# Attention, then two gated layers, on one core: first loads in one queue, weights' clamp on GpSimd, weight steps counted by eight

## The chip, the core and the metric

The kernel runs on one core of a Trainium2 chip. The time is that of one execution in microseconds on the device, the median of 3 runs. The engines are called as in the profile: PE (TensorE, matmuls), DVE (VectorE), ACT (ScalarE), POOL (GpSimd), SP (SyncE, which only issues transfers here). POOL issues transfers too, in its own queue.

## What is computed

```python
# attention with decay: B, H, S, D = 4, 8, 768, 64, one gamma for each head
for t in range(S):
    state = gamma * state + k[:, :, t] (outer) v[:, :, t]
    y[:, :, t] = scale * q[:, :, t] @ state
x = y as 3072 tokens x 512
# first layer: w1, w2 512x1024, w3 1024x1024, w_out 1024x512
x = ((x @ w1) * (x @ w2)) @ w3 @ w_out
# second layer: w_in 512x2048, w_out 2048x512
h = x @ w_in
out = (h * sigmoid(1.702 * h)) @ w_out
```

q, k, v are float32, all weights float64.

## The kernel before

**Attention** runs over 24 chunks of 128 tokens, 6 for each of 4 sequences (class `Attention`). A chunk's q, k, v are one tile, 1.05 MB, loaded by POOL's queue (`load`); there are four such tiles, so the load for chunk c + 4 waits until chunk c is done with its own. For a chunk PE computes scores `s`, the state's update `u` and the output `y` (from the masked scores `pt`, and from the state where there is one). ACT scales v into `vs`; DVE masks the scores into `pt` and multiplies y by a decay factor `dy` into `xb`. The factors of chunk 0 are loaded, those of the other five places come from POOL as products (`factors`). The first four chunks stay in SBUF, split by ACT and DVE into a high and a low part (`xh`, `xl`); the others are stored (`xd`). Tile `y` has one buffer.

**Weights** come as float64, in halves of a tile, 0.52 MB each (`fetch`, tile `raw`, five buffers), and are turned on the chip into a float32 high and low part. That is a generator, `weight_steps`, one instruction of DVE to a step. For a tile: two clamps (L168), the two low parts of the tile ahead (L118), two shifts left (L175), two or-steps with the lower word (L179), two and-steps that set the sign (L188). ACT makes the magnitudes (`magnitude`, L109) and the high parts (L113). When an and-step has read a raw half for the last time, the next half is fetched. `PAIR_OPS` is the count of steps to a tile.

**The order** is written out by hand: `tc.manual_schedule` keeps each engine's instructions as the program gives them, and an engine that waits holds up all that is behind it in its queue. `run` walks over the chunks and calls `fill(c, at)` at four places in each; `fill` takes `OPS[...][at]` weight steps, 3 to a chunk until the four tiles of `w_out` and the first of `w3` are made, then 8. From then on it also puts a *mix block* behind a chunk's output, where a tile of w3 is ready: 24 matmuls (tile `psw`) that multiply one of 8 blocks of w3 with w_out in advance. Mix blocks that are left are done when attention has ended. The gate stage (tile `psm`, w1 and w2) comes next, and then the rest.

Of the kernel before, what the change touches and what calls it, by code (L numbers as in the profile page):

```python
# [9 lines left out]
I32 = mybir.dt.int32  # L10
AF = mybir.ActivationFunctionType
ALU = mybir.AluOpType
# [6 lines left out]
NCK = S // P  # L19
NC = B * NCK  # L20
# [6 lines left out]
R_BUFS = 5  # L27
# [5 lines left out]


LEAST, MOST = 2.0, (1 + 0x680000 / 2**23) * 2.0**32
PAIR_OPS = 10

OPS = (1, 0, 1, 1), (2, 2, 2, 2)

# [2 lines left out]
def tile_kernel(  # L42
# [14 lines left out]
    nc = tc.nc  # L57
# [26 lines left out]
    raws, wx, parts = {}, {}, {}  # L84
# [4 lines left out]
            homes[tag].tile([P, 1024], F32R, tag=tag, bufs=8, name=f"w{x}") for x in "hl"  # L89
        )  # L90

    def fetch(n):

        i, c = divmod(n, 2)
        if i >= len(tiles):
            return
        src = tiles[i][0][:, c * WC : (c + 1) * WC].bitcast(I32)
        raw = prep.tile([P, WC, 2], I32, tag="r", bufs=R_BUFS, name="raw")
        nc.sync.dma_start(raw, src.rearrange("p (c w) -> p c w", w=2))
        raws.setdefault(i, []).append(raw)  # L100

    def magnitude(i):
        if i >= len(tiles):
            return
        wx[i] = []
        for raw in raws[i]:
            x = prep.tile([P, WC], F32, tag="x", bufs=4, name="x")
            high = raw[:, :, 1].bitcast(F32)
            nc.scalar.activation(x, high, AF.Abs, scale=2.0**16)  # L109
            wx[i].append(x)  # L110

    def upper(i, n):
# [49 lines left out]
    def weight_steps():  # L162

        for i in range(len(tiles)):
            if i == 0:
                magnitude(i)
            for x in wx[i]:
                nc.vector.tensor_scalar(x, x, LEAST, MOST, ALU.max, ALU.min)  # L168
                yield i - 1
            for k, low in enumerate(lows):  # L170
                low()
                yield i - (k < len(lows) - 1)
            for x in wx[i]:
                bits = x.bitcast(I32)
                nc.vector.tensor_scalar(bits, bits, 3, None, ALU.logical_shift_left)  # L175
                yield i
            for x, raw in zip(wx[i], raws[i]):
                bits = x.bitcast(I32)
                nc.vector.scalar_tensor_tensor(  # L179
                    bits, raw[:, :, 0], 29, bits, ALU.logical_shift_right, ALU.bitwise_or  # L180
                )
                yield i
            magnitude(i + 1)
            if i < WI:
                parts[i] = wtile(tiles[i][1])
            for n, (x, raw) in enumerate(zip(wx[i], raws[i])):
                bits = x.bitcast(I32)
                nc.vector.scalar_tensor_tensor(  # L188
                    bits, raw[:, :, 1], -(2**31), bits, ALU.bitwise_and, ALU.bitwise_or
                )  # L190
                if i < WI:
                    upper(i, n)
                fetch(2 * i + n + R_BUFS)
                yield i
            if i < WI:
                lows[:] = [lambda i=i, n=n: lower(i, n) for n in range(2)]
            else:
                for _ in seven(i):
                    yield i
        for low in lows:  # L200
            low()
            yield i + 1
# [4 lines left out]
    def work(n):  # L207

        nonlocal complete, done
        for _ in range(n):  # L210
            complete = next(steps, len(tiles))
            done += 1
# [34 lines left out]
    class Attention:  # L247
# [121 lines left out]
        def run(self, fill):  # L369

            self.scores(0)
            self.masked(0)
            for c in range(NC):
                if c + 1 < NC:
                    self.scores(c + 1)
                fill(c, 0)
                if c + 1 < NC:
                    self.masked(c + 1)
                fill(c, 1)
                self.updates(c)  # L380
                self.next_state(c)
                if c + 3 < NC:
                    self.load(c + 3)
                if c + 2 in range(2, NCK):
                    self.factors(c + 2)
                fill(c, 2)
                self.outputs(c)
                fill(c, 3)


# [311 lines left out]
    with tc.manual_schedule():  # L702
        with (
# [3 lines left out]
            attention = Attention(p0, ps0)  # L707
            nc.sync.dma_start(attention.dv, cv)
            nc.sync.dma_start(attention.mask, cmask)
            fetch(0)  # L710
            attention.load(0)
            fetch(1)
            attention.load(1)
            nc.sync.dma_start(attention.step[:, :NCK], cstep)
            attention.factors(0)
            attention.load(2)
            attention.factors(1)
            for n in range(2, R_BUFS):
                fetch(n)
            psw = None  # L720
            halves_done = 0

# [30 lines left out]

            def fill(c, at):
                nonlocal usable
                work(OPS[usable > W3][at])
                mix_out()
                if at == 3 and W3 + halves_done // 2 < min(usable, W12):
                    mix_half()
                    mix_half()  # L760
                usable = complete

            work(3)
            attention.run(fill)
            while halves_done < 2 * KF:
                f = halves_done // 2
# [220 lines left out]
```

## Time and profile before

| | us |
|---|---|
| runs | 1027.65, 1027.82, 1028.16 |
| median | 1027.82 |
| the profiled execution | 1028.51 |
| its span, first to last instruction | 1026.7 |
| PE busy in it | 991.8 (97%) |
| DVE, ACT, POOL busy | 647.6, 441.8, 46.1 |

The profile is of one execution. A line of the timeline merges neighbours of one kind (x2: two instructions); what stands in brackets is the idle time of the engine just before, and what ended it. DMA share is the mean busy share of the 16 DMA engines, PEclk the granted clock of PE, 1.00 being full speed.

### The profile page before, as it was taken

What the parts mean: (1) busy time and instruction counts of PE and PEld (TensorE: products, weight loads), DVE (VectorE), ACT (ScalarE), POOL (GpSimd) and SP (SyncE); (2) the same over time, 40 slices, a digit from 0 to 9 for tenths busy, and PEclk for the clock granted to TensorE, in tenths of its full rate; (3) what the DMA queues carried; (4) which work ended last, traced back from release to release, by engine and by line L of the source; (5) the groups of instructions that cost most, each with busy time, mean ns of one, the idle gap of its engine ahead of it and who ended that gap; (6) DMA issues with size and microseconds to landing.
All of it is one profiled execution on the core that took longest, in us unless ns stands there. A gap on an engine that the chain in (4) does not pass through costs nothing.

```text
span 1026.7 us, 16851 instructions
## 1 busy us (share of the span) xinstructions
PE 991.8 (97%) x6688; PEld 900.1 (88%) x6688; DVE 647.6 (63%) x1048; ACT 441.8 (43%) x875; POOL 46.1 (4%) x65
## 2 busy tenths in 40 slices
PE   4879999999999999999999999999999999999997
PEld 3668777888888888888889999999999999999997
DVE  4877888856767777742442362634646588687782
ACT  4767544433434434322113455555455343433431
POOL 3110000000000000000001000000001011011011
PEclk9999999999999999999999999999999999999999
DMA  8999645436676666650137925233469854344331
GB/s 310 336 400 361 239 155 177 151 125 220 230 269 201 223 238 215 219 177 16 55 131 313 372 96 181 102 132 151 150 220 416 330 165 162 110 138 142 106 123 41
DMA packets 80159, 202.79 MB, mean 198 GB/s; under 512 B 6736, under 2 KB 33488, under 8 KB 75088
## 3 DMA queue, kind: packets, MB, share of 16 engines
q1 hardware_dynamic: 73888, 146.14, 40.8%
q0 software_dynamic: 6192, 55.58, 13.8%
q8 instruction: 52, 0.85, 0.3%
q14 instruction: 27, 0.22, 0.1%
HBM read 129.34 MB, written 72.35 MB: 196 GB/s over the span
## 4 chain that ended last, share of the span: by engine, by line
PE 87%; DMA 6%; DVE 4%; issue 1%; ACT 1%; POOL 0%; DVEq 0%; ACTq 0%; POOLq 0%
PE psm L225 8%; PE psm L224 8%; PE psm L223 8%; PE m L223 8%; PE m L225 8%; PE m L224 8%; PE acc L224 4%; PE acc L223 4%; PE acc L225 4%; DMA qkv<-in_qkv_dram 4%; PE a L223 4%; PE a L224 4%; PE a L225 4%; PE e L223 2%; PE e L224 2%; PE e L225 2%
## 5 line engine op out<-in xcount | busy, mean ns | idle before, releaser
L223 PE MATMUL m<-oh,op 128*128 128x256 f32 x672 | 188.2, 280 | 0.0
L225 PE MATMUL m<-oh,op 128*128 128x256 f32 x672 | 187.6, 279 | 0.0
L224 PE MATMUL m<-ol,op 128*128 128x256 f32 x672 | 187.6, 279 | 0.0
L225 PE MATMUL psm<-xh,wl 128*128 128x512 f32 x384 | 149.5, 389 | 1.2 <-DVE wl L118 1.2
L224 PE MATMUL psm<-xl,wh 128*128 128x512 f32 x384 | 149.4, 389 | 0.0
L223 PE MATMUL psm<-xh,wh 128*128 128x512 f32 x384 | 149.4, 389 | 0.0
L225 PEld LDWEIGHTS m<-oh,op 128*128 128x128 f32 x672 | 126.4, 188 | 0.0
L223 PEld LDWEIGHTS m<-oh,op 128*128 128x128 f32 x672 | 126.3, 188 | 0.0
L224 PEld LDWEIGHTS m<-ol,op 128*128 128x128 f32 x672 | 125.8, 187 | 0.0
L819 DVE TENSOR_TENSOR tmp<-tmp,psm 128x512 f32<-128x512 f32 x48 | 32.9, 686 | 103.9 <-PE psm L225 92.9
L225 PEld LDWEIGHTS psm<-xh,wl 128*128 128x128 f32 x384 | 72.1, 188 | 16.5 <-DVE wl L118 1.6
L223 PE MATMUL a<-yh,op 128*128 128x384 f32 x256 | 85.6, 335 | 0.6 <-ACT u L472 0.6
L597 ACT CAST oh<-gr 128x512 fp32r<-128x512 f32 x69 | 38.3, 618 | 111.1 <-issue 53.4
L225 PE MATMUL a<-yh,op 128*128 128x384 f32 x256 | 85.5, 334 | 0.0
L224 PE MATMUL a<-yl,op 128*128 128x384 f32 x256 | 85.5, 334 | 0.0
L223 PEld LDWEIGHTS psm<-xh,wh 128*128 128x128 f32 x384 | 72.1, 188 | 15.0
L224 PEld LDWEIGHTS psm<-xl,wh 128*128 128x128 f32 x384 | 72.1, 188 | 14.9
L800 ACT CAST hh<-tmp 128x512 fp32r<-128x512 f32 x48 | 29.8, 621 | 124.4 <-DVE tmp L819 124.4
L223 PE MATMUL acc<-hh,wh 128*128 128x512 f32 x192 | 74.7, 389 | 0.0
L224 PE MATMUL acc<-hl,wh 128*128 128x512 f32 x192 | 74.7, 389 | 0.0
L225 PE MATMUL acc<-hh,wl 128*128 128x512 f32 x192 | 74.7, 389 | 0.0
L510 DVE TENSOR_TENSOR s<-c,s 128x384 f32<-128x384 f32 x32 | 17.8, 557 | 83.5 <-PE c L225 79.3
(106 smaller groups left out, 1899.7 us busy)
## 6 DMA issues: line engine op xcount, KB each, us to landing
op<-sp POOLq DMA_DIRECT2D x16, 1792.0 KB, 10.6
gd<-g SPq DMA_DIRECT2D x64, 384.0 KB, 2.5
qkv<-in_qkv_dram POOLq DMA_DIRECT2D x23, 1024.0 KB, 8.2
raw<-in_w_dram SPq DMA_DIRECT2D x32, 512.0 KB, 4.7
gr<-gd SPq DMA_DIRECT2D x30, 512.0 KB, 4.7
raw<-in_wo_dram SPq DMA_DIRECT2D x24, 512.0 KB, 5.7
raw<-in_wi_dram SPq DMA_DIRECT2D x16, 512.0 KB, 4.6
sp<-wqh SPq DMA_DIRECT2D x16, 512.0 KB, 3.4
```

The costliest lines, as they stand in the source:

```text
L223: nc.tensor.matmul(ps, wh, xh, start=start, stop=False, skip_group_check=True)
L224: nc.tensor.matmul(ps, wh, xl, start=False, stop=False, skip_group_check=True)
L225: nc.tensor.matmul(ps, wl, xh, start=False, stop=stop, skip_group_check=True)
L510: nc.vector.tensor_tensor(s1, c, s1, ALU.add)
L597: nc.scalar.copy(h, x)
L800: nc.scalar.copy(hi, t)
L819: nc.vector.tensor_tensor(t, t, pb, ALU.mult)
```

## The change

- The first loads: the constants stay on SP, now with the factors `step` and `dy` right behind the mask. The first four chunks' q, k, v and the first five raw halves of the weights go through POOL's queue, in turns, ahead of all else there. Before, the raw halves were on SP's queue, and chunk 3's load stood behind the first product of factors.
- `load(c + 4)` is called behind `outputs(c)`; before, `load(c + 3)` behind `next_state(c)`.
- The clamp of the magnitudes goes from DVE to POOL, right behind ACT's magnitude. A tile then takes 8 steps of DVE, in the order shifts, low parts of the tile ahead, or-steps, and-steps. `PAIR_OPS` is 8.
- The first three weight steps are called behind chunk 0's scores and masks (`fill(0, -1)`); before, ahead of attention. So ACT scales chunk 0's v ahead of the first magnitudes.

```diff
-PAIR_OPS = 10
+PAIR_OPS = 8
...
-    def fetch(n):
+    def fetch(n, queue=nc.sync):
...
-        nc.sync.dma_start(raw, src.rearrange("p (c w) -> p c w", w=2))
+        queue.dma_start(raw, src.rearrange("p (c w) -> p c w", w=2))
...
             nc.scalar.activation(x, high, AF.Abs, scale=2.0**16)
+            nc.gpsimd.tensor_scalar(x, x, LEAST, MOST, ALU.max, ALU.min)
...
             for x in wx[i]:
-                nc.vector.tensor_scalar(x, x, LEAST, MOST, ALU.max, ALU.min)
+                bits = x.bitcast(I32)
+                nc.vector.tensor_scalar(bits, bits, 3, None, ALU.logical_shift_left)
                 yield i - 1
             for k, low in enumerate(lows):
                 low()
                 yield i - (k < len(lows) - 1)
-            for x in wx[i]:
-                bits = x.bitcast(I32)
-                nc.vector.tensor_scalar(bits, bits, 3, None, ALU.logical_shift_left)
-                yield i
...
             self.masked(0)
+            fill(0, -1)
...
-                if c + 3 < NC:
-                    self.load(c + 3)
                 if c + 2 in range(2, NCK):
                     self.factors(c + 2)
                 fill(c, 2)
                 self.outputs(c)
+                if c + 4 < NC:
+                    self.load(c + 4)
...
-            fetch(0)
+            nc.sync.dma_start(attention.step[:, :NCK], cstep)
             attention.load(0)
-            fetch(1)
+            fetch(0, nc.gpsimd)
+            attention.factors(0)
             attention.load(1)
-            nc.sync.dma_start(attention.step[:, :NCK], cstep)
-            attention.factors(0)
+            fetch(1, nc.gpsimd)
             attention.load(2)
+            fetch(2, nc.gpsimd)
+            attention.load(3)
+            for n in range(3, R_BUFS):
+                fetch(n, nc.gpsimd)
             attention.factors(1)
-            for n in range(2, R_BUFS):
-                fetch(n)
...
             def fill(c, at):
                 nonlocal usable
+                if at < 0:
+                    work(3)
+                    return
...
-            work(3)
             attention.run(fill)
```

Line numbers shift a little with the change. Three places show what moves.

POOL's queue from the start of the program. Before (`qkv` are the loads, `dy` the products of factors):

```order
L272 DMA qkv<-in_qkv_dram 128x1024 x2
L272 DMA qkv<-in_qkv_dram 128x2048 x2
L265 ISA
L265 TENSOR_TENSOR dy<-dy,step 128x512
L272 DMA qkv<-in_qkv_dram 128x2048
L265 TENSOR_TENSOR dy<-dy,step 128x512
L272 DMA qkv<-in_qkv_dram 128x2048
L265 TENSOR_TENSOR dy<-dy,step 128x512
L272 DMA qkv<-in_qkv_dram 128x2048
L265 TENSOR_TENSOR dy<-dy,step 128x512
```

After, from the first product of factors on (ahead of it stand the loads of chunks 0 to 3 and five raw halves; L110 is the clamp):

```order
L263 TENSOR_TENSOR dy<-dy,step 128x512
L110 TENSOR_SCALAR x<-x 128x512 x2
L263 TENSOR_TENSOR dy<-dy,step 128x512
L110 TENSOR_SCALAR x<-x 128x512 x2
L270 DMA qkv<-in_qkv_dram 128x2048
L263 TENSOR_TENSOR dy<-dy,step 128x512
L270 DMA qkv<-in_qkv_dram 128x2048
L263 TENSOR_TENSOR dy<-dy,step 128x512
L270 DMA qkv<-in_qkv_dram 128x2048
L110 TENSOR_SCALAR x<-x 128x512 x2
L263 TENSOR_TENSOR dy<-dy,step 128x512
L270 DMA qkv<-in_qkv_dram 128x2048 x3
```

The load of chunk 3 has moved to the front, and clamps stand between the products and the loads; those of the third tile are ahead of the load of chunk 7.

PE at the end of attention. Before, one of the last chunks, between two mix blocks:

```order
L225 MATMUL psw<-wh,wl 128x512
L290 MATMUL s<-qkv 128x128 x8
L316 MATMUL u<-vs,qkv 64x64 x8
L340 MATMUL y<-pt,vs 64x128 x8
L350 MATMUL y<-qkv,state_111 64x128 x8
L223 MATMUL psw<-wh 128x512
```

After, from the end of the last mix block to the first gate matmul:

```order
L223 MATMUL psw<-wh,wl 128x512
L288 MATMUL s<-qkv 128x128 x8
L314 MATMUL u<-vs,qkv 64x64 x8
L338 MATMUL y<-pt,vs 64x128 x8
L348 MATMUL y<-qkv,state_112 64x128 x8
L288 MATMUL s<-qkv 128x128 x8
L314 MATMUL u<-vs,qkv 64x64 x8
L338 MATMUL y<-pt,vs 64x128 x8
L348 MATMUL y<-qkv,state_111 64x128 x8
L338 MATMUL y<-pt,vs 64x128 x8
L348 MATMUL y<-qkv,state_112 64x128 x8
L221 MATMUL psm<-xh,wh 128x512
```

Mix blocks stand behind chunks 16, 17, 18, 20, 21 and 22 before, and two behind the last chunk; after, behind chunks 13 to 20, and none behind the last three.

DVE at the same place. Before, from the low part of chunk 22's mix block (L750) to past the last `xb`:

```order
L750 TENSOR_TENSOR wl<-psw,wh 128x512
L168 TENSOR_SCALAR x<-x 128x512 x2
L118 TENSOR_TENSOR wl<-x,wh 128x512 x2
L362 TENSOR_TENSOR xb<-y,dy 128x512
L175 TENSOR_SCALAR x<-x 128x512 x2
L179 SCALAR_TENSOR_TENSOR x<-raw,x 128x512 x2
L188 SCALAR_TENSOR_TENSOR x<-raw,x 128x512 x2
L168 TENSOR_SCALAR x<-x 128x512 x2
L118 TENSOR_TENSOR wl<-x,wh 128x512 x2
L175 TENSOR_SCALAR x<-x 128x512 x2
L179 SCALAR_TENSOR_TENSOR x<-raw,x 128x512 x2
```

After, from the low part of the last mix block (L751) to `xb` of chunk 22:

```order
L751 TENSOR_TENSOR wl<-psw,wh 128x512
L300 TENSOR_TENSOR pt<-s,mask 128x512 x2
L186 SCALAR_TENSOR_TENSOR x<-raw,x 128x512 x2
L170 TENSOR_SCALAR x<-x 128x512 x2
L360 TENSOR_TENSOR xb<-y,dy 128x512
L119 TENSOR_TENSOR wl<-x,wh 128x512 x2
L177 SCALAR_TENSOR_TENSOR x<-raw,x 128x512 x2
L300 TENSOR_TENSOR pt<-s,mask 128x512 x2
L186 SCALAR_TENSOR_TENSOR x<-raw,x 128x512 x2
L170 TENSOR_SCALAR x<-x 128x512 x2
L360 TENSOR_TENSOR xb<-y,dy 128x512
```

The last mix block's low part comes two chunks earlier, and eight weight steps stand in each of these chunks with no mix block beside them.

## Rows read from the trace of the kernel before

**Rows 1.** Busy time by stage: stretch, length, then the columns of the first row.

```profile
core 0: us, PE busy (x) PEld busy (x) DVE busy (x) ACT busy (x) POOL busy (x), PEclk, DMA share, GB/s
24.00:42.00 18.00, 14.33 (x228) 11.95 (x229) 15.28 (x27) 11.41 (x37) 3.09 (x5) 0.91 0.87 328
42.00:74.10 32.10, 26.58 (x481) 22.46 (x480) 27.35 (x50) 24.11 (x88) 4.54 (x8) 0.95 1.00 388
74.10:88.00 13.90, 11.07 (x192) 9.56 (x192) 10.35 (x19) 8.87 (x31) 1.58 (x3) 0.88 0.96 361
88.00:138.00 50.00, 48.75 (x487) 38.80 (x480) 39.95 (x77) 29.46 (x81) 2.36 (x4) 1.00 0.72 257
138.00:165.00 27.00, 25.43 (x134) 19.91 (x134) 23.35 (x46) 11.54 (x20) 0.00 (x0) 1.00 0.51 176
165.00:600.00 435.00, 434.52 (x1986) 368.20 (x1985) 260.07 (x467) 161.64 (x285) 4.23 (x8) 1.00 0.54 194
```

**Rows 2.** TensorE's list of waits, 0 to 170 us: total us, times, longest.

```profile
PE s L290 <- DMA qkv<-in_qkv_dram: 22.5, 6, 8.3
```

**Rows 3.** Timeline, POOL and PE at the start: start us, us, engine, what.

```profile
16.94 1.44 POOL L265 TENSOR_TENSOR dy<-dy,step 128x512 f32<-128x512 f32 x1 [13.40 <-DMA dy<-in_cy_dram]
...
18.33 0.59 POOL L272 DMA_DIRECT2D qkv<-in_qkv_dram  x1
...
25.07 1.16 PE L290 MATMUL s<-qkv 64*128 64x128 f32 x16 [3.00 <-DMA qkv<-in_qkv_dram]
...
33.67 0.59 POOL L272 DMA_DIRECT2D qkv<-in_qkv_dram  x1 [1.50 <-ACT state L328]
```

**Rows 4.** Timeline of DVE and POOL, 23 to 32 us.

```profile
23.07 1.27 DVE L302 TENSOR_TENSOR pt<-s,mask 128x512 f32<-128x512 f32 x2
...
23.27 1.05 POOL L265 TENSOR_TENSOR dy<-dy,step 128x512 f32<-128x512 f32 x1
...
31.11 1.05 POOL L265 TENSOR_TENSOR dy<-dy,step 128x512 f32<-128x512 f32 x1
...
31.43 1.29 DVE L240 TENSOR_TENSOR xl<-xb,xh 128x512 fp32r<-128x512 f32 x1 [0.68 <-ACT xh L239]
```

**Rows 5.** Timeline of DVE over one weight tile, 142 to 148 us.

```profile
142.74 0.69 DVE L750 TENSOR_TENSOR wl<-psw,wh 128x512 fp32r<-128x512 f32 x1 [1.97 <-ACT wh L749]
...
143.35 0.75 DVE L168 TENSOR_SCALAR x<-x 128x512 f32<-128x512 f32 x2
...
144.01 1.29 DVE L118 TENSOR_TENSOR wl<-x,wh 128x512 fp32r<-128x512 f32 x2
...
145.22 0.68 DVE L362 TENSOR_TENSOR xb<-y,dy 128x512 f32<-128x512 f32 x1
...
145.82 0.75 DVE L175 TENSOR_SCALAR x<-x 128x512 int32<-128x512 int32 x2
...
146.49 1.28 DVE L179 SCALAR_TENSOR_TENSOR x<-raw,x 128x512 int32<-128x512 int32 x2
```

**Rows 6.** Timeline of TensorE, 74 to 88 us.

```profile
76.93 1.57 PE L290 MATMUL s<-qkv 64*128 64x128 f32 x16 [2.84 <-DMA qkv<-in_qkv_dram]
...
81.69 1.16 PE L290 MATMUL s<-qkv 64*128 64x128 f32 x16
...
84.87 1.16 PE L290 MATMUL s<-qkv 64*128 64x128 f32 x16
```

**Rows 7.** Timeline of TensorE, 127 to 156 us.

```profile
127.46 0.50 PE L223 MATMUL psw<-wh 128*128 128x512 f32 x1
...
136.33 0.50 PE L223 MATMUL psw<-wh 128*128 128x512 f32 x1
...
142.01 1.09 PE L340 MATMUL y<-pt,vs 128*64 128x128 f32 x16
...
143.64 0.50 PE L223 MATMUL psw<-wh 128*128 128x512 f32 x1
...
155.42 0.39 PE L223 MATMUL psm<-xh,wh 128*128 128x512 f32 x1
```

## The prediction

> **What bounds the kernel now.** I read the busy time by stage first [rows 1]. From 165 us on TensorE (PE) is busy all the time (434.52 of 435 us), in the same program order before and after, so the change can move the end only by when that stretch starts. Ahead of it three stages differ. From 24 to 74.1 us PE has gaps and the DMA engines do not (share 0.87, then 1.00 at 388 GB/s): attention chunks wait for their q, k, v. The list of waits says the same: 22.5 us of PE's waiting is for the qkv loads, in 6 waits [rows 2]. From 88 to 138 us PE is full, because the mixing of w3 with w_out (tile psw, 24 matmuls for each of its 8 blocks) stands between the chunks. From 138 to 165 us DVE prepares weights (23.35 of 27 us busy) while PE works off the last two mix blocks; little is lost there.
>
> So I price the change at two points. The first is the end of chunk 13's output at 74.1 us, T13 from here on: in the new order the first mix block stands there, three chunks earlier than now. The second is the first gate matmul (tile psm), now at 155.42 us [rows 7], behind which PE stays full. The sum is made against the profiled execution, 1028.51 us with its span of 1026.7, which lies 0.7 us above the median of 1027.82; I take the 0.7 off at the end.
>
> **The change, part by part.**
>
> *A, what the earlier mixing saves.* A weight tile costs DVE 10 steps now and 8 after (the pair of clamps, 0.75 us [rows 5], leaves). The number of steps per chunk stays 3, so the fifth tile is ready three chunks sooner and the mixing starts behind chunk 13 instead of 16. With a mix block in it a chunk takes PE 8.87 us (from 127.46 to 136.33 [rows 7]) and asks for about 2.4 MB (1.05 MB of q, k, v, 0.26 MB stored, a tile of 1.05 MB); at 388 GB/s [rows 1] that is 6.1 us, so the DMA waits behind T13 go. What PE loses there now is idle time of 2.83, 1.25 and 1.57 us in the three stages after 74.1 us [rows 1], 5.65 together. To it comes the low clock after the wait of 2.84 us: that chunk takes 4.76 us (76.93 to 81.69), the next 3.18 (to 84.87) [rows 6], 1.6 more; the granted clock of that stage is 0.88, the lowest of all, which mixes PE's level of 2.4 GHz with a while at 1.2 after the wait. **A = -7.2 us** if all of it goes; at least the 2.84 and the 1.6 should.
>
> *B, what the new end of attention costs.* All 8 mix blocks are then used up behind chunk 20, and chunks 21, 22 and 23 have none between them, while DVE still does 8 weight steps in each. PE's output of chunk 23 waits for DVE's xb of chunk 22, since tile y has one buffer. From the first matmul of the last mix block: its low part starts on DVE 6.41 us later (136.33 to 142.74 [rows 5, 7]). From there to the end of that xb DVE has one row of the mix, two pairs of masks, of and-steps, of shifts, one pair of low parts, one of or-steps, and two xb: 0.69 + 2 x (1.28 + 1.28 + 0.75 + 0.68) + 1.29 + 1.28 = 11.2 us, with the durations of [rows 5], the pair of masks from [rows 4], the and-steps (L188) taken like the or-steps (L179). Then come 1.63 us of chunk 23's output (142.01 to 143.64 [rows 7]): 19.3 us. PE's own work in it is the mix block (8.87 - 3.18 = 5.7), two chunks of 3.18 and the 1.63, 13.7 us. It idles **5.6 us**, most of it in one piece ahead of chunk 23, so I add the low clock behind such a wait, 1.6 us as in [rows 6]. I also add 0.8 us for the clamps (next part). **B = +8.0 us**; 5.6 without clock and clamps, 11.4 if all four clamps in that stretch block DVE for 1.05 us each.
>
> *The clamps on GpSimd (POOL).* No row shows this operation there. The nearest is POOL's product of the same 128x512, 1.05 us [rows 4]. It has two inputs, so I take 1.05 as a ceiling that is likely and 0.42 (half of DVE's 0.75 for two, with the 0.05 of a single row) as a floor. That row also shows what POOL does to DVE: the low part of x (L240, both inputs in SBUF) started at 31.43 while POOL worked from 31.11 to 32.16, and took 1.29 us, where a row of that kind takes 0.64 (half of the L118 pair [rows 5]). It did its work after POOL had ended. The masks at 23.07, which read PSUM, took the usual 1.27 for two beside POOL's row at 23.27. So a clamp blocks DVE's weight steps and not its masks or xb. In the mix stage the clamps fall largely under the mix's low part and the masks; I take 0.4 us lost per pair out of 0 to 2.1. DVE then has 0.69 + 1.28 + 0.68 + 4.6 (the tile's 8 steps) = 7.25 us per chunk and 0.4 more, under PE's 8.87: hidden there, paid in B alone.
>
> The Trainium skill, page SBUF — State Buffer, section "SBUF: two separate sides", calls the port that DVE and GpSimd share an exclusive lock: the one that starts second is blocked for the whole instruction. The 1.29 us row agrees. By that rule the move is no gain of 0.75 us per tile but a trade. GPSIMD Engine Reference, section "3.1 Elementwise", has 769 ns for a one-input loop of 512 elements; no row here shows it. By it a pair could block DVE for at most 1.5 us, and B would end at 10.3.
>
> *C, when T13 comes.* Three things. (1) 3 steps of 8 instead of 3 of 10 per chunk fetch 0.075 tile more, 0.079 MB, over 13 chunks 1.0 MB; at 388 GB/s 2.6 us, as the DMA is full from 42 us on [rows 1]. (2) POOL's queue. Asking four chunks ahead changes nothing by itself: there are four buffers, and each load already goes out when the chunk four before it is done. But the clamps now stand in that queue ahead of loads: load 7, out at 33.67 now [rows 3], stands behind the clamps of the third tile, which wait for ScalarE's magnitudes, which stand behind the scaled v of chunk 4 there. By the rows around it that is some 4 us later; DMA has 13% to spare in that stage (18 us x 0.13 = 2.3 us), and I take +1.0 (0 to 2.3). (3) The start. POOL waited 13.40 us for dy, so load 3 went out at 18.33 and chunk 3 waited 3.00 us [rows 3]. dy now comes early and load 3 goes out with the first ones, in front of the last weights. Against that, DVE's masks of chunk 1 now stand behind two shifts and two or-steps of the first tile, which wait for clamps, magnitudes and the second raw weights; and ScalarE's first cast of x stands behind the magnitude of the fourth raw piece, which is the second but last of ten transfers. Of the 3.0 us I keep 1.1 (-1.5 to 3.0). **C = 2.6 + 1.0 - 1.1 = +2.5 us**, between -3.0 (start kept, nothing else) and +6.4.
>
> The rest costs nothing: the later tiles' clamps come in a stretch where PE is full and DVE is busy 260 of 435 us [rows 1]; that is its cover, and DVE enters it about two tiles further ahead than now.
>
> **Sum:** -7.2 + 8.0 + 2.5 = +3.3; 1028.5 + 3.3 - 0.7 = **1031.1 us**.
>
> **The rivals.**
>
> *R1, not slower, the start carries through.* If the first loads bring chunk 3's 3.0 us and the extra weights fit into the DMA's gaps before 42 us, C is -3.0 and T13 is at 71; A and B stay: -2.2, or 1025.6. If the clock also holds in B it is 1024. For it: 3.00 us of wait at one load [rows 3]. Against it: DVE's order puts weight work ahead of chunk 1's masks. It decides where T13 comes before 71.2 us.
>
> *R2, it cancels.* The extra megabyte goes into the gaps of 24 to 42 us (2.3 us worth, [rows 1]), and start and late load cancel: C = 0, +0.8, so 1028.6. For it: the share of 0.87 there. Against it: 1.00 right behind it.
>
> *R3, the lock.* Each clamp blocks DVE for its 1.05 us: a chunk of the mix stage takes DVE 7.25 + 2.1 = 9.35 us, over PE's 8.87, and 7 chunks lose 0.5 each, 3.4 us; B grows by 3.4 too. With C as above: 1037.9. It decides from 1.6 us of blocking per pair (8.87 - 7.25). Against it: masks and mix rows, which POOL does not block, stand where the clamps fall.
>
> **How the numbers follow.** About 0.2%, 2 us, is what a measurement of this kernel can tell from no change: the borders are 1025.8 and 1029.9. The forecast (1030 to 1034) gets 0.43, R3 (1034 to 1040) 0.10, R2 (1026 to 1029.9) 0.27, R1 (1023 to 1025.8) 0.20. So faster 0.20, same 0.27, slower 0.53. The range leaves out the low part of R1 and most of R3, about 0.17: 1025 to 1036.5. The terms are of both signs and each as large as the result, hence its width.
>
> **What would show it.** A: no wait of PE for qkv once the first psw has run, and psw between chunks from 13 on. B: PE idle for 5 to 6 us between the last psw and the first psm, released by DVE, with the granted clock low behind it. C: the end of chunk 13's output at 76 to 77 us (R1: before 71.2, R2: 74). Clamps: the mean of POOL's clamp rows, and DVE's low and or-steps over 0.68 us on average. I am wrong if PE goes from the last psw to psm without that gap, or if T13 moves by more than 4 us.

## The result: 0.97% slower

| | us |
|---|---|
| the changed kernel, 4 runs | 1037.67, 1037.92, 1037.97, 1038.89 |
| median | 1037.95 |
| the kernel before, 4 runs beside it, median | 1027.99 |
| ratio, with its 95% interval | 1.0097 (1.008 to 1.0115) |
| the profiled execution, its span | 1037.67, 1035.9 |

The forecast was 1031.1 with a range up to 1036.5. The sign was right and the time was not: the loss is about 10 us instead of 3.3, and outside the range. It is also, to 0.1 us, the time that rival R3 gave; the trace shows that it came in another way.

### The profile page after: what moved, and what is told of

It is laid out like the page before. It is cut to its first block, busy times and chain, and to the rows that moved or that the text cites. A ratio compares the mean times of both kernels' runs of the same rounds, so it can differ in the third digit from the quotient of the medians.

```text
span 1035.9 us, 16875 instructions
## 1 busy us (share of the span) xinstructions
PE 999.5 (96%) x6688; PEld 906.6 (88%) x6688; DVE 646.3 (62%) x976; ACT 442.5 (43%) x875; POOL 207.8 (20%) x142
## 4 chain that ended last, share of the span: by engine, by line
PE 91%; DMA 3%; DVE 2%; ACT 1%; POOL 1%; issue 1%; DVEq 0%; POOLq 0%; ACTq 0%
PE psm L221 8%; PE psm L222 8%; PE psm L223 8%; PE m L221 8%; PE m L223 8%; PE m L222 7%; PE a L221 4%; PE a L222 4%; PE a L223 4%; PE acc L222 4%; PE acc L221 4%; PE acc L223 4%; PE e L222 2%; PE e L221 2%; PE e L223 2%; PE psw L221 2%
## 5 line engine op out<-in xcount | busy, mean ns | idle before, releaser
L110 POOL TENSOR_SCALAR x<-x 128x512 f32<-128x512 f32 x72 | 160.1, 2237 | 204.1 <-ACT x L109 201.3
L803 ACT CAST hh<-tmp 128x512 fp32r<-128x512 f32 x48 | 29.8, 621 | 132.8 <-DVE tmp L822 132.8
L455 POOL DMA_DIRECT2D op<-sp x16 | 8.6, 535 | 387.1 <-PE a L223 206.1
```

Source lines behind the costliest of these rows:

```text
L110: nc.gpsimd.tensor_scalar(x, x, LEAST, MOST, ALU.max, ALU.min)
L455: nc.gpsimd.dma_start(t.rearrange("p a b c -> p a (b c)").bitcast(F32), sp[n])
L803: nc.scalar.copy(hi, t)
```

## The profile after

Busy time by stage, the same stretches as in [rows 1], same columns:

```profile
24.00:42.00 18.00, 14.25 (x198) 11.77 (x194) 15.35 (x23) 12.77 (x42) 7.70 (x8) 0.80 0.72 251
42.00:74.10 32.10, 25.12 (x376) 21.43 (x378) 26.78 (x43) 20.72 (x73) 13.22 (x13) 0.79 0.92 344
74.10:88.00 13.90, 12.75 (x160) 10.30 (x156) 12.85 (x23) 10.19 (x32) 9.36 (x7) 1.00 1.01 386
88.00:138.00 50.00, 50.00 (x488) 40.19 (x488) 40.66 (x71) 30.90 (x86) 29.78 (x18) 1.00 0.89 289
138.00:165.00 27.00, 20.26 (x246) 16.43 (x244) 23.81 (x41) 14.54 (x38) 13.25 (x8) 0.92 0.61 202
165.00:600.00 435.00, 435.00 (x1986) 366.94 (x1983) 253.69 (x412) 155.82 (x270) 97.39 (x48) 1.00 0.53 191
```

TensorE's list of waits up to 170 us, the answer to [rows 2]:

```profile
PE s L288 <- DMA qkv<-in_qkv_dram: 14.2, 4, 6.2
PE s L288 <- DVE pt L300: 7.4, 4, 3.5
PE y L338 <- DVE xb L360: 6.3, 2, 5.1
PE u L314 <- ACT state L326: 1.3, 3, 0.7
```

Two lines of the same list before the change, for comparison:

```profile
PE s L290 <- DVE pt L302: 1.9, 2, 1.1
PE psm L225 <- DVE wl L118: 1.2, 1, 1.2
```

The stage from 88 to 138 us is full, 50.00 of 50 us against 48.75. From 24 to 74.1 us the DMA is no longer full (0.72 and 0.92 against 0.87 and 1.00), and in the whole list the loads' waits have fallen from 22.5 to 14.2 us. Two waits for DVE have come instead: 7.4 us for masks `pt`, all ahead of the first mix block, where 1.9 us were waited before, and 6.3 us for `xb`, all behind the last one. TensorE's clock from 24 to 74.1 us is 0.80 and 0.79, against 0.91 and 0.95 before.

Rows of TensorE's timeline that answer to [rows 7]: the first mix block, the last one, the two long waits behind it, and the first gate matmul.

```profile
83.17 0.50 PE L221 MATMUL psw<-wh 128*128 128x512 f32 x1
```

```profile
144.13 0.50 PE L221 MATMUL psw<-wh 128*128 128x512 f32 x1
...
156.53 1.09 PE L338 MATMUL y<-pt,vs 128*64 128x128 f32 x16 [1.23 <-DVE xb L360]
...
163.28 1.98 PE L338 MATMUL y<-pt,vs 128*64 128x128 f32 x16 [5.06 <-DVE xb L360]
165.19 1.13 PE L348 MATMUL y<-qkv,state 64*64 64x128 f32 x16
166.25 0.80 PE L221 MATMUL psm<-xh,wh 128*128 128x512 f32 x1
```

With these the span divides into three parts:

| | before | after | difference | forecast |
|---|---|---|---|---|
| start to the end of chunk 13's output | 74.1 | 83.2 | +9.1 | C = +2.5 |
| from there to the first gate matmul | 81.3 | 83.1 | +1.8 | A + B = +0.8 |
| from there to the end | 871.3 | 869.7 | -1.6 | 0 |

So nearly all of the miss stands before 83 us. The page's group of the clamp (its columns: count, busy, mean ns, idle before it and the releaser of that) and rows of POOL, DVE and PE at the clamps of the first two tiles:

```profile
L110 POOL TENSOR_SCALAR x<-x 128x512 f32<-128x512 f32 x72 | 160.1, 2237 | 204.1 <-ACT x L109 201.3
```

```profile
14.21 1.91 POOL L110 TENSOR_SCALAR x<-x 128x512 f32<-128x512 f32 x1 [1.53 <-ACT x L109]
...
16.15 1.25 DVE L170 TENSOR_SCALAR x<-x 128x512 int32<-128x512 int32 x1 [3.02 <-POOL x L110]
...
18.53 1.28 DVE L300 TENSOR_TENSOR pt<-s,mask 128x512 f32<-128x512 f32 x2
...
19.27 1.16 PE L288 MATMUL s<-qkv 64*128 64x128 f32 x14 [1.51 <-DVE pt L300]
...
22.03 1.92 POOL L110 TENSOR_SCALAR x<-x 128x512 f32<-128x512 f32 x1 [1.64 <-ACT x L109]
...
23.89 0.62 POOL L270 DMA_DIRECT2D qkv<-in_qkv_dram  x1
...
24.21 3.26 DVE L170 TENSOR_SCALAR x<-x 128x512 int32<-128x512 int32 x1
...
24.53 1.05 POOL L263 TENSOR_TENSOR dy<-dy,step 128x512 f32<-128x512 f32 x1
...
26.13 1.05 POOL L263 TENSOR_TENSOR dy<-dy,step 128x512 f32<-128x512 f32 x1
...
27.40 1.28 DVE L300 TENSOR_TENSOR pt<-s,mask 128x512 f32<-128x512 f32 x2
...
28.13 2.07 PE L288 MATMUL s<-qkv 64*128 64x128 f32 x14 [3.45 <-DVE pt L300]
```

A clamp takes 1.9 us at the least and 2.24 on average, not 1.05. The first tile's second clamp ends at 16.12; only then does DVE's shift run, which stands in front of chunk 1's masks (18.53), for which PE waits until 19.27. The load of chunk 4 goes out at 23.89, behind the second tile's clamps, though the last matmul that reads its buffer, the state's update of chunk 0, ends at 15.38 us. Then DVE's shift takes 3.26 us instead of 0.42: it lies beside two of POOL's products of factors and ends 0.3 us behind the second. Behind it come the next masks, and PE waits 3.45 us for them; that wait is not one for the clamp.

## The experiments

Every ratio is to runs of the kernel before on the same chip. "The end of a chunk" is the end of its output on TensorE, read from the rows of `y`. T13 is that of chunk 13, as in the prediction. Times are medians; what is read from a trace is of one execution, and that lies up to 2.2 us from the median of its run, and 4.8 in one case, which is named. So differences of 1 to 2 us between two traces show little.

| end of chunk, us | 0 | 1 | 2 | 6 | 9 | 13 |
|---|---|---|---|---|---|---|
| before | 18.3 | 22.1 | 29.9 | 45.2 | 58.6 | 74.1 |
| the change | 17.1 | 24.1 | 34.0 | 52.7 | 69.1 | 83.2 |
| clamp on DVE | 16.9 | 20.2 | 25.4 | 42.7 | 55.9 | 71.5 |
| no clamp | 16.1 | 20.0 | 30.0 | 45.7 | 58.5 | 75.2 |
| shifts late | 17.3 | 25.4 | 34.8 | 54.5 | 65.9 | 84.8 |
| loads on SP | 17.0 | 25.1 | 29.6 | 48.9 | 64.4 | 81.8 |
| shifts late, loads on SP | 16.6 | 24.1 | 32.4 | 50.7 | 64.2 | 80.4 |
| clamp alone | 29.8 | 33.4 | 37.9 | 61.3 | 78.7 | 106.0 |

### Which part of the change costs

**Clamp on DVE, in the step order of the kernel before, the rest of the change kept.**

```diff
-PAIR_OPS = 8
+PAIR_OPS = 10
...
-            nc.gpsimd.tensor_scalar(x, x, LEAST, MOST, ALU.max, ALU.min)
...
             for x in wx[i]:
-                bits = x.bitcast(I32)
-                nc.vector.tensor_scalar(bits, bits, 3, None, ALU.logical_shift_left)
+                nc.vector.tensor_scalar(x, x, LEAST, MOST, ALU.max, ALU.min)
                 yield i - 1
...
+            for x in wx[i]:
+                bits = x.bitcast(I32)
+                nc.vector.tensor_scalar(bits, bits, 3, None, ALU.logical_shift_left)
+                yield i
```

> The change without its clamp: the clamp is DVE's again (two more steps, 10 to a tile), the new first loads, the load four chunks ahead and the first weight steps behind chunk 0's masks stay. Mixing starts behind chunk 16 again, so terms A and B both go. Theory W (the clamp of 1.92 us on POOL, for which DVE's shifts wait with the masks of the next chunk behind them, made the 9.1 us by which chunk 13 ends later): the loss goes with the clamp, 1024 to 1029 us, chunk 13 ends at 71 to 75 us. Theory Q (the loads, all in POOL's queue and in the new order, make it): most of the loss stays, 1032 to 1037 us, chunk 13 ends after 79.

1025.52 us, ratio 0.9962 (0.9944 to 0.998): faster than before. T13 is at 71.5. The new first loads are no loss, so theory Q falls.

**No clamp at all.**

```diff
-            nc.gpsimd.tensor_scalar(x, x, LEAST, MOST, ALU.max, ALU.min)
```

> The change with the clamp left out altogether (the clamp is not computed); 8 steps of DVE to a tile, in the order of the change, and the mixing behind chunk 13 stay. Theory W: chunk 13 ends at 74 to 77 us as forecast, DVE's shifts wait for nothing, the end stretch still costs B; 1027 to 1031 us. Theory Y (bytes: 8 steps to a tile fetch weights faster, and that takes the DMA from q, k, v): the loss stays, chunk 13 ends after 80 us, 1034 to 1038 us.

1029.94 us, ratio 1.0014 (1.0000 to 1.0027). T13 is at 75.2, and the first gate matmul at 156.2. So the clamp on POOL makes the loss, as theory W says, and Y falls; by which wait it does so this run doesn't show. The 8 steps to a tile, with A, B, the bytes and the start in it, cost 1.4 us (0 to 2.8); the clamp on POOL costs the other 8.5 (1.0097 less 1.0014).

**The clamp alone, in the kernel before.**

```diff
-PAIR_OPS = 10
+PAIR_OPS = 8
...
+            nc.gpsimd.tensor_scalar(x, x, LEAST, MOST, ALU.max, ALU.min)
...
             for x in wx[i]:
-                nc.vector.tensor_scalar(x, x, LEAST, MOST, ALU.max, ALU.min)
+                bits = x.bitcast(I32)
+                nc.vector.tensor_scalar(bits, bits, 3, None, ALU.logical_shift_left)
                 yield i - 1
...
```

> The kernel before with the clamp alone on POOL (8 steps, order of the change); first loads, loads three ahead and first weight steps in front as before. Theory W: slower, 1034 to 1039 us, as the whole change. Theory Q: the loss lies in the loads, so this is 1027 to 1031 us, A and B nearly cancelling.

1059.25 us, ratio 1.0296 (1.0277 to 1.0316), far worse than either theory had it. Its timeline at the start, on POOL, DVE and PE:

```profile
16.97 1.03 POOL L263 TENSOR_TENSOR dy<-dy,step 128x512 f32<-128x512 f32 x1 [13.42 <-DMA dy<-in_cy_dram]
17.99 3.80 POOL L110 TENSOR_SCALAR x<-x 128x512 f32<-128x512 f32 x2
19.95 0.83 DVE L170 TENSOR_SCALAR x<-x 128x512 int32<-128x512 int32 x1 [19.95 <-POOL x L110]
...
24.99 2.07 PE L288 MATMUL s<-qkv 64*128 64x128 f32 x14 [10.68 <-DVE pt L300]
```

There the first clamps stand in POOL's queue behind the first product, which waits for `dy` until 16.97; DVE's first shift waits for them until 19.95, and the masks of chunk 0 wait behind it, PE with them for 10.68 us. The new first loads and the moved first steps in the change remove that wait: of the 30 us which the clamp, with the 8 steps to a tile, costs alone, they take away 20.

**The first three weight steps in front again** (with the clamp on DVE).

```diff
-            fill(0, -1)
...
+            work(3)
             attention.run(fill)
```

> The first loads of the change, clamp on DVE, and the first three weight steps ahead of attention again, as before; it takes the move of these steps out of the 0.9962. If the move is what brings the gain (ScalarE scales the first v without waiting for the first raw weights), 0.998 to 1.001 and chunk 0's output some 3 us later. If the order of the first loads brings it, 0.995 to 0.998.

1028.92 us, ratio 1.0003 (0.9991 to 1.0015). Chunk 0 ends at 20.5 us rather than 16.9, and the first mix block starts at 90.3 rather than 85.8. So the gain of the version with the clamp on DVE hangs on the moved first steps; the new loads without them bring none. The moved steps without the new loads were not tried.

### How the clamp costs

**One operation instead of two** (the upper bound isn't computed).

```diff
-            nc.gpsimd.tensor_scalar(x, x, LEAST, MOST, ALU.max, ALU.min)
+            nc.gpsimd.tensor_scalar(x, x, LEAST, None, ALU.max)
```

> The change with a clamp of one operation instead of two (only the lower bound; the upper bound is not computed). If POOL's 1.92 us is the price of two operations in one pass, the row is some 1.0 us, near the 1.05 that the product of factors takes and that the prediction took, and the time shows what the mis-sized row cost: 1.003 to 1.006. If the row stays near 1.9 us, the price is the form (one input and a scalar) and the time stays at 1.008 to 1.010.

1035.21 us, ratio 1.0063 (1.0045 to 1.0081). POOL's first two rows of it:

```profile
10.68 1.49 POOL L110 TENSOR_SCALAR x<-x 128x512 f32<-128x512 f32 x1 [0.72 <-ACT x L109]
14.50 1.48 POOL L110 TENSOR_SCALAR x<-x 128x512 f32<-128x512 f32 x1 [2.33 <-ACT x L109]
```

It takes 1.48 us: neither of the two values expected. The second operation costs 0.44 us, and with 0.44 us less for each clamp the kernel is some 3.5 us faster than the change, with intervals that only just touch. The price of the row matters, but even at one operation it isn't 1.05.

**Shifts behind the low parts,** so that the clamp has two more DVE steps to be done in.

```diff
-            for x in wx[i]:
+            for low in lows:
+                low()
+                yield i - 1
+            for n, x in enumerate(wx[i]):
                 bits = x.bitcast(I32)
                 nc.vector.tensor_scalar(bits, bits, 3, None, ALU.logical_shift_left)
-                yield i - 1
-            for k, low in enumerate(lows):
-                low()
-                yield i - (k < len(lows) - 1)
+                yield i - (n == 0)
```

> The change with the two low parts ahead of the two shifts in each tile's steps, so that two more DVE steps lie between ScalarE's magnitude and the first step that needs the clamp. The mixing starts at the same chunk. If the wait in DVE's order is the cause (W), a good part of it goes: DVE waits for POOL less than half of the 18.7 us before 165 us, 1030 to 1034 us. If POOL's clamp costs by blocking DVE or by holding the loads behind it in POOL's queue, the order of the steps changes little: 1036 to 1039 us.

1036.48 us, ratio 1.0081 (1.0061 to 1.01). Up to 165 us DVE waits 6.3 us for POOL's clamps instead of 18.7, and T13 doesn't come earlier: 84.8, in an execution 2.0 us above the median. DVE's wait as a sum isn't the cost.

**Loads from chunk 4 on issued by SP,** away from the clamps.

```diff
-        def load(self, c):
+        def load(self, c, queue=nc.gpsimd):
...
-                nc.gpsimd.dma_start(t[:, slice(*h)], qkv[c][:, slice(*h)])
+                queue.dma_start(t[:, slice(*h)], qkv[c][:, slice(*h)])
...
-                    self.load(c + 4)
+                    self.load(c + 4, nc.sync)
```

> The change with the loads of q, k, v from chunk 4 on issued by SP, so that they no longer stand behind the clamps in POOL's queue (behind raw halves and stores on SP instead). Theory H (the clamp costs its 8 us because loads whose buffer is free stand behind it in POOL's queue: load 4 was held 6.9 us, load 7 5.4, load 12 3.8): the first mix block starts at 75 to 79 us rather than 83.2, 1029 to 1034 us. Theory K (the clamp costs by occupying POOL and so blocking DVE, wherever the loads are): the first mix block stays at 82 or later, 1036 to 1039 us. A rival of its own: loads behind raw halves and stores on SP are held as long as behind the clamps, and it is no better for that reason; then load issues on SP stand later than their buffer is free.

1037.14 us, ratio 1.0087 (1.0064 to 1.011): no gain that can be told. The first mix block starts at 81.7. The rival named there is part of it, at one load at least: on SP load 7 goes out at 37.73 us, behind a raw half at 37.24, where its buffer was done with at 34.6.

**Both of these together.**

> Both waits for the clamp lightened at once: the low parts ahead of the shifts (1.0081 alone) and the loads from chunk 4 on issued by SP (1.0087 alone, against 1.0097 for the whole change). If the clamp costs by two waits side by side, DVE's steps with the masks behind them and the loads behind the clamp, and each alone keeps chunk 13 late, then the two together give much more than their sum: ratio 1.002 to 1.005, first mix block at 76 to 80 us. If it is POOL's occupation that costs, or if loads on SP are held as long there, they add up at most: 1.006 to 1.009, first mix block at 81 or later.

1034.43 us, ratio 1.0056 (1.0036 to 1.0076), between the two expectations. By the medians it takes 4 us off the 1.0097, where the two alone take 1.6 and 1.0; the intervals allow a plain sum too. T13 is 80.4.

**The clamp on a tile that nobody waits for.**

```diff
-            nc.gpsimd.tensor_scalar(x, x, LEAST, MOST, ALU.max, ALU.min)
+            if i < 16:
+                nc.gpsimd.tensor_scalar(
+                    spare[0], dyt[0].rearrange("p n t -> p (n t)"), LEAST, MOST, ALU.max, ALU.min
+                )
...
+            spare.append(attention.tile("spare", KD * P, 1))
```

> The change with the clamp done on another tile: POOL does an operation of the same form and size at the same places, for the first 16 weight tiles, but it reads a factor tile that is there from the start and nobody waits for its result (the weights are left unclamped). So POOL neither waits for ScalarE's magnitudes nor does DVE wait for POOL; what is left of the clamp's cost is POOL's 1.92 us each and what it blocks. Theory H: the loads are held by at most 3.8 us for a pair and mostly not at all, since POOL can run ahead of ScalarE: 1029 to 1032 us, the first mix block at 75 to 77. Theory K: the blocking stays, 1034 to 1038 us, the first mix block at 80 or later.

1031.95 us, ratio 1.0036 (1.0018 to 1.0054), against 1.0014 without any clamp. Its profiled execution was the slowest of nine, 1036.73, so its trace is not read for sizes; the first mix block came at 83.6 in it, as late as in the change, so that the 75 to 77 us expected for it are not shown. By the medians POOL's work and what it blocks are worth 2 us or so of the 8.5, with an interval that reaches from nothing to 4; the larger part, 6.3 of the 8.5, is waiting for the clamp.

**More work for TensorE in its waits,** to see whether its clock is the cause. Busy time by stage from the start to T13, the kernel before and the change (columns as in [rows 1]):

```profile
0.00:74.10 74.10, 51.58 (x832) 43.71 (x832) 52.18 (x90) 46.78 (x155) 16.60 (x28) 0.95 0.93 347
```

```profile
0.00:83.17 83.17, 59.59 (x832) 49.78 (x832) 57.71 (x89) 50.27 (x160) 42.97 (x46) 0.86 0.87 322
```

The idle time is nearly the same, 22.5 and 23.6 us; the same 832 matmuls take 59.6 us instead of 51.6, at a mean granted clock of 0.86 instead of 0.95, a mixture of the levels 2.4 and 1.2 GHz.

```diff
+            if 0 < c <= 13:
+                t = self.ps.tile([P, DM], F32, tag="w", bufs=2, name="warm")
+                for _ in range(16):
+                    nc.tensor.matmul(t[:, :P], self.mask[:, 0], self.mask[:, 0], ...)
```

> The change with 16 more matmuls of 128x128 (the mask with itself, the result unused) ahead of the scores of chunks 1 to 13, so that TensorE works in a part of its waits. If the low clock sets the end of chunk 13, the clock up to there rises from 0.86 to 0.95 or more and the first mix block comes at 76 to 80 us rather than 83.2, although some 15 us of matmuls are added: ratio 1.002 to 1.007. If it only fills time in which TensorE would wait, the added work costs or nothing changes: first mix block at 83 or later, 1.009 to 1.016.

1057.85 us, ratio 1.0289: the dose was 3.84 us a chunk, 50 us in all, and TensorE became the bound (94.9 us busy up to the first mix block at 102.5). With a quarter of it (`range(4)`):

> The change with 4 more matmuls (8 passes, 0.96 us at full clock) ahead of the scores of chunks 1 to 13, 12.5 us of added work in all, against 23.6 us of waits up to chunk 13's end. If the low clock sets that end, the clock rises to 0.95 or more there and the first mix block comes at 77 to 81 us in spite of the added work: ratio 1.003 to 1.007. If the low clock only fills time in which TensorE would wait anyway, the first mix block stays at 82 to 86 and the ratio at 1.008 to 1.012. If the added work is itself on the path, it is later than that.

1037.36 us, ratio 1.0095 (1.0073 to 1.0116). Busy time, clock and DMA share of this kernel from the start to 82 us, 1 us ahead of its first mix block at 82.96:

```profile
0.00:82.00 82.00, 65.01 (x916) 55.63 (x918) 57.17 (x88) 49.41 (x160) 41.49 (x46) 0.96 0.87 326
```

The clock rises from 0.86 to 0.96 and the first mix block stays at 83.0. That alone doesn't settle it, since the 12.5 us of added work can have cost what the clock gave back. Another run settles it without added work. The kernel with fewer weight steps behind the last mix block (the next section) is the change's own program up to chunk 20, and in its profiled execution the clock was higher:

```profile
0.00:83.00 83.00, 55.79 (x832) 46.35 (x832) 57.90 (x89) 50.20 (x160) 43.07 (x46) 0.92 0.88 324
```

The same matmuls take 55.8 us there instead of 59.6, and the first mix block comes at 83.05 instead of 83.17. So the low clock by itself doesn't set T13; what the matmuls gain, TensorE waits longer instead (27.2 us idle against 23.6).

### The end of attention, and a better version

**Fewer weight steps behind the last mix block** (in the change).

```diff
-OPS = (1, 0, 1, 1), (2, 2, 2, 2)
+OPS = (1, 0, 1, 1), (2, 2, 2, 2), (1, 0, 1, 1)
...
-                work(OPS[usable > W3][at])
+                work(OPS[2 if halves_done == 2 * KF else usable > W3][at])
```

> The change with 3 instead of 8 weight steps in a chunk once the eight mix blocks are used up (chunks 21 to 23), a test of term B alone. If the end stretch costs what it was put at (waits for DVE's xb of 5.06 and 1.23 us and the low clock behind), it gives 6 to 9 us back: 1029 to 1032 us, first gate matmul at 157 to 160 us rather than 166.25. If the steps only move behind the last chunk (the gate stage asks for tile 13 before its first output), it gives under 2 us: 1036 to 1038 us.

1034.42 us, ratio 1.0059 (1.004 to 1.0078). The first gate matmul comes at 158.8 rather than 166.25, 7.4 us earlier, as expected; the end of the profiled execution is only 3.8 us earlier. TensorE's list of waits (to 1040 us) says where most of the rest went:

```profile
PE psm L223 <- DVE wl L119: 2.7, 4, 0.8
```

The gate stage waits for low parts which DVE had made in the stretch that was lightened; the change has no such wait. Half of the gain is given back behind the first gate matmul, 2.7 of the 3.6 us in these waits.

**Mixing earlier with the clamp on DVE:** 4 steps in a chunk, then 10, then 3.

```diff
-OPS = (1, 0, 1, 1), (2, 2, 2, 2)
+OPS = (1, 1, 1, 1), (2, 3, 2, 3), (1, 0, 1, 1)
...
-                work(OPS[usable > W3][at])
+                work(OPS[2 if halves_done == 2 * KF else usable > W3][at])
```

> The first loads of the change with the clamp on DVE (10 steps), and the steps dealt out anew: 4 in a chunk until the fifth tile is ready, 10 in a chunk with a mix block, 3 in the chunks behind the last one. It has term A without B and without POOL's clamp. By the sum so far (term A is worth what it was put at, B is avoidable): first mix block at 74 to 78 us, first gate matmul at 148 to 153, 1019 to 1024 us. Rival: 4 steps in a chunk make DVE the bound before the mix starts, or 10 in a mix chunk over PE's 8.87; then 1025 to 1029 us, with PE waiting for DVE.

1026.74 us, ratio 0.9976 (0.9962 to 0.9989), a gain within the rival's range. The first mix block comes at 73.7 us, but the first gate matmul at 157.8. At full speed a chunk takes 3.18 us [rows 6]: 13 chunks were done at 73.7, so 73.7 less 41.3, 32.4 us, had been lost by then; with the clamp on DVE alone it was 17 chunks at 85.8, 31.7 us. (The trace is of its slowest execution, 1028.89.) In these two traces mixing earlier doesn't by itself save anything ahead of the first mix block, and behind the last one this version loses 2.6 and 1.1 us to waits for DVE and ScalarE.

**Ten steps from chunk 16 on, clamp on DVE:**

```diff
-OPS = (1, 0, 1, 1), (2, 2, 2, 2)
+OPS = (1, 0, 1, 1), (2, 3, 2, 3)
```

> The first loads of the change, clamp on DVE, and 10 instead of 8 weight steps in a chunk once the mixing has begun (at chunk 16), so that a tile of w3 is ready for each chunk. Expected: first mix block at 85 to 87 us as with the clamp on DVE, no wait of TensorE for a low part in the mix stage or at the start of the gate stage (1.2 us each before), ratio to before 0.993 to 0.996, a little under the 0.9962 with 8 steps. If 10 steps make DVE the bound in a mix chunk (8.0 us of 8.87 by its rows, and ScalarE's casts wait for it), TensorE waits for masks or xb there and it is 0.996 to 1.000.

1024.20 us, ratio 0.9956 (0.9942 to 0.997): the best, and faster than both kernels. It can't be told from 0.9962. The waits for low parts in the mix stage are gone, the one at the start of the gate stage isn't (1.5 us). The same with 8 added matmuls ahead of the scores of chunks 1 to 13:

> The version with the first loads of the change, clamp on DVE and 10 steps in a mix chunk (ratio 0.9956), with 8 such matmuls ahead of the scores of chunks 1 to 13. There the clock is 0.98 up to chunk 13's end and the DMA is full behind 50 us, so the loads set it: no gain, 0.995 to 0.999. If the two stretches with a clock of 0.83 (60 to 80 us) cost, 0.991 to 0.994.

1029.22 us, ratio 1.0007 (0.9992 to 1.0023). The clock is 1.00 throughout and the time 5 us longer: here the added work costs more than the clock gives.

## Why the prediction was wrong

*What bounds the kernel* held: from 166 us on TensorE is full (435.00 of 435 us from 165), so T13 and the start of the gate stage decide nearly all of it, and the miss is found there. By its own sign, T13 moving by more than 4 us, the prediction is wrong: T13 moved by 9.1.

*A* was right. Behind the first mix block there is no wait for q, k, v, and TensorE is full from 83.2 us to the end of the last block (68.80 of 68.8 us up to 152). From T13 to the first gate matmul the change is +1.8; with B's 8.1 us ahead of that matmul A is, by subtraction, -6.3, forecast -7.2. Only its reading as the profit of mixing earlier is too simple, as the run with early mixing showed.

*B* was right. The last mix block's first matmul is at 144.13 and its low part runs at 150.55 us, 6.42 later (forecast 6.41). TensorE then waits 0.45, 1.23 and 5.06 us, 6.7 against 5.6, and the output behind the wait of 5.06 runs at 1.98 and 1.13 us instead of 1.09 and 0.67, the level of 1.2 GHz after a wait, as the first gate matmul does with 0.80 instead of 0.39 [rows 7]: 6.7 and 1.4, 8.1 us ahead of that matmul, forecast 8.0. In the DVE rows of that stretch each tile's second shift waits 1.06 us for POOL.

*The rest at nothing* was too careful: from the first gate matmul to the end the change takes 1.6 us less. 1.2 of it is the wait for a low part that the kernel before had there and that is gone with DVE further ahead; the other 0.4 isn't accounted for. The run with a lighter end shows the same from the other side.

*C failed.* Its bytes and its start together came to +1.1 (T13 75.2 without the clamp, in an execution 1.9 us below that run's median, so up to 3), forecast 2.6 - 1.1 = 1.5: near, but from other parts. Of the start nothing was kept, where 1.1 had been counted: it was gained with the clamp on DVE (chunk 2 at 25.4) and lost again with 8 steps to a tile (30.0, against 29.9 before). The reason is one that the prediction named and priced too low. In the version without a clamp the magnitude of the fourth raw half waits for its load in front of the cast of x; DVE's low part of x waits for the cast, and TensorE for the masks behind it:

```profile
20.83 0.67 ACT L109 ACTIVATE x<-raw 128x512 f32<-128x512 f32 x1 [3.09 <-DMA raw<-in_wo_dram]
...
21.90 0.62 ACT L236 CAST xh<-xb 128x512 fp32r<-128x512 f32 x1
...
22.55 0.69 DVE L237 TENSOR_TENSOR xl<-xb,xh 128x512 fp32r<-128x512 f32 x1 [4.30 <-ACT xh L236]
...
24.84 2.07 PE L287 MATMUL s<-qkv 64*128 64x128 f32 x14 [4.43 <-DVE pt L299]
```

What failed is the price of the clamp, in two steps. First, "I take 1.05 as a ceiling that is likely": the ceiling was a row of another operation, and the clamp takes 1.92. The price was looked for only in what it blocks. Second, the waiting for it was costed with +1.0 for load 7 (0 to 2.3) and, for the masks, inside a start that was still a gain. Load 4 stood behind clamps too, for 8.5 us (15.38 to 23.89); without a clamp it goes out as soon as the state's update of chunk 0 is done:

```profile
15.42 0.59 POOL L269 DMA_DIRECT2D qkv<-in_qkv_dram  x1 [4.57 <-PE u L313]
```

And chunk 1 ended at 24.1 instead of 20.0 because its masks stood behind shifts that waited. Against the version without a clamp chunk 1 is already 4.1 us late, and chunk 13 is 8.0.

What the clamp blocks was near the forecast, and small. POOL's and DVE's rows at the third tile's clamps, and two from a later pair:

```profile
38.03 3.93 POOL L110 TENSOR_SCALAR x<-x 128x512 f32<-128x512 f32 x2 [2.83 <-DVE pt L300]
...
38.48 0.70 DVE L186 SCALAR_TENSOR_TENSOR x<-raw,x 128x512 int32<-128x512 int32 x1
...
40.47 0.69 DVE L238 TENSOR_TENSOR xl<-xb,xh 128x512 fp32r<-128x512 f32 x1 [0.69 <-ACT xh L237]
...
41.07 0.42 DVE L170 TENSOR_SCALAR x<-x 128x512 int32<-128x512 int32 x1
...
59.56 4.12 POOL L110 TENSOR_SCALAR x<-x 128x512 f32<-128x512 f32 x2 [1.75 <-ACT x L109]
...
61.83 0.83 DVE L170 TENSOR_SCALAR x<-x 128x512 int32<-128x512 int32 x1
```

An and-step, a low part of x with both inputs in SBUF and a shift lie inside the clamps (38.03 to 41.96) and take their usual 0.70, 0.69 and 0.42 us. Others beside a clamp are longer, like the shift at 61.83, but by 0.4 us and not by the clamp's 1.9. Up to 165 us the means of DVE's or-steps, and-steps and shifts are 0.72, 0.74 and 0.64 us, against 0.71, 0.68 and 0.42 before, so a pair of clamps costs DVE 0.6 us, the products' share in it; 0.4 had been taken out of 0 to 2.1. What stretches a step most is the two-input product (the 3.26 us above). By the Trainium skill, page SBUF — State Buffer, section "SBUF: two separate sides", an operation of DVE with two SBUF inputs and a GpSimd operation that reads SBUF exclude each other for the whole instruction. Beside the product the low part of x at 31.43 in [rows 4] agrees, with 1.29 us; beside the clamp the and-step at 38.48 and the low part of x at 40.47, both with two SBUF inputs, don't: neither waited for the end of the clamp. The shift of 3.26 us has one input, so that this sentence doesn't cover it.

*R3* gave 1037.9 and the time is 1037.95, but its place is not there: it had the mix stage lose 3.4 us, and that stage is full; it had each clamp block DVE for 1.05 us, and a pair costs it 0.6. It is a right number from a wrong mechanism. *R1* and *R2* needed T13 at 71 or 74.

What stays open: how the 8 us before T13 divide between masks behind shifts and loads behind clamps. Each, lightened alone, gave 1 to 1.6 us, both together 4, and what they leave (1.0056 against 1.0014) isn't accounted for. TensorE's own waits don't decide it: from 20 us to T13 it waits 4.0 us for loads and 5.9 for masks in the trace of the change, 7.5 and 6.4 in that of the lighter end, which is the same program up to there.

## What to carry to other kernels

- Work that is moved to another engine's queue can be paid in two places where that queue also issues loads: price what stands behind it there, and what stands behind its consumer in the consumer's order, for each time it occurs and not for one.
- A duration bounded by a row of another operation is no ceiling. Where the whole sum rests on it, keep a wide range: here the operation took 1.8 times the row.
- Work that is taken out of a stretch to shorten it may have been feeding the next one: here 3.6 of 7.4 us were lost again, 2.7 of them as waits in the gate stage.

## What was not expected of the hardware

- POOL's clamp of 128x512 float32 takes 1.48 us with one operation and 1.92 with two, its two-input product 1.05.
- Beside two products a shift of DVE took 3.26 us instead of 0.42; steps of DVE inside a clamp took their usual time or 0.4 us more, not the clamp's 1.9.
- The same 832 matmuls take 59.6 us at a mean clock of 0.86, 55.8 at 0.92 and 51.6 at 0.95. Between the first two, two executions of the same program up to that point, the end of chunk 13 differs by 0.1 us.
